# Moving an attention block from one chunk's down phase into the next chunk's up phase, with one cast on GpSimd

## Chip, cores and metric

One Trainium2 chip, one core. The metric is the device time of one execution in microseconds (us), the median of the runs. TensorE is called PE, VectorE DVE, ScalarE ACT, GpSimd POOL and SyncE SP, as in the profile.

## What is computed

```python
def _attn_ref(q, k, v):                       # (8, 8, 576, 64) each
    scores = scale * np.matmul(q, k.transpose(0, 1, 3, 2))
    gamma = 1.0 - 2.0 ** (-5.0 - np.arange(H))
    rel = pos[:, None] - pos[None, :]
    Dmat = np.where(rel >= 0, gamma[:, None, None] ** rel[None, :, :], 0.0)
    return np.matmul(scores * Dmat[None], v)

def _moe_ref(x, w_in, w_out):                 # x (4608, 512), w_in (512, 2048), w_out (2048, 512)
    h = x @ w_in
    g = h * (1.0 / (1.0 + np.exp(-1.702 * h)))
    return (g @ w_out)

x = attn_out.transpose(0, 2, 1, 3).reshape(B * S, H * D)
out = _moe_ref(x, w_in, w_out)
```

Attention has a decay per head in place of a softmax, so a sequence can be walked in pieces of 64 tokens with a running state (the sum of k times v). Its output, 4608 tokens of 512 features, goes through a two-layer network with a gate function between the layers.

## The kernel before

**Units, blocks, chunks.** A unit is 128 tokens with all 8 heads; there are 36. Every ninth unit (8, 17, ...) holds the last 64 tokens of two sequences and updates no state. Two units, 2j and 2j+1, make attention block j. Four units make a chunk, which the network takes at a time; there are 9 chunks. Chunk c needs x of blocks 2c and 2c+1.

**Attention of a block.** `scores` (L505) multiplies keys and queries into the PSUM banks C and D; `scores_out` (L514) masks them on DVE into `pm`. `state_both` (L434) forms the state updates of both halves of a unit in the banks K and E; `state_sum` (L447, L449) adds them up on DVE in `stm` (float32), and `state_cast` (L458) turns them into bf16 in `kv`. `block(j)` then runs `inter` (L489: queries times `kv`) and the first half of `values` (L527: `pm` times the scaled values `vp`), calls `ahead(j + 1)` (the scores and states of the next block), and runs the second half of `values`. It hands back a list of DVE steps to be issued later: `x_out_pair` (L552, which writes x in `xT`) for block j, and the masks and state sums for block j+1. `scale_v` (L353) makes `vp` on DVE.

**Network of a chunk.** The up phase has 16 steps f: `up` (L564) is 4 matmuls of 512 columns, then the gate function on ACT (L569) into `gT`; the banks A and B take turns. `up_group` does two f for half a chunk (units `lo` to `hi`): 8 matmuls of 256 columns (L578), one gate call (L583). `Pair.sums` (L653, L657) adds and subtracts parts of `gT` on DVE, 5 instructions for 8 f. The down phase is `Pair.run`: seven products of 16 matmuls (L675) on the banks A and B, with copies out on ACT (L691) and additions on DVE (L694), and seven places, `hook(0)` to `hook(6)`, where `steady` issues attention work.

**Order.** Each engine runs its instructions in the order of the program, and a small recorder puts semaphore waits between engines. So `steady` writes the order by hand: what is issued at which hook or step decides what waits behind what. In the up phase of chunk c it issues block 2c+2 and in the down phase block 2c+3. Chunk 1 is different: its up phase runs in half-chunk groups and holds block 3, and its down phase holds blocks 4 and 5, both of chunk 2:

```python
if i == 3:
    now(rest); rest.clear(); cast_now()
    rest.extend(block(4, cast=False))
if i == 5:
    now(rest); rest.clear(); state_cast(10, 12)
    rest.extend(block(5, cast=False))
n = len(rest) if i == 6 else 2
now(rest[:n])
```

**Loads.** GpSimd issues the loads of q, k (cast to bf16 on the way, `kqn`, L234) and v (`vn`, L247). SP issues the stores (L600) and the DMA transposes of `kqn` into `kqT` (L399). At the start of chunk c the transposes of units 4c+6 to 4c+9 are issued on SP, and the loads of units 4c+10 to 4c+13 on GpSimd, these after the transpose of unit 4c+9 has landed.

Of the kernel before, what the change touches and what calls it, by code (L numbers as in the profile page):

```python
# [29 lines left out]
class Program:  # L30
# [10 lines left out]
    def op(self, eng, fn, reads=(), writes=(), dma=None, ndma=1, after_ops=()):  # L41
        o = Op()
        o.eng, o.fn, o.dma, o.signal, o.count = eng, fn, dma, False, None
        o.idx = len(self.streams[eng]) + 1
        deps = {}
        for k in reads:
            for d in self.writers.get(k, ()):
                deps[id(d)] = (d, True)
        for k in writes:
            for d in self.writers.get(k, ()) + self.readers.get(k, ()):  # L50
                deps.setdefault(id(d), (d, False))
        known = self.known[eng]
        need = []
        for d, raw in deps.values():
            if d.dma is None:
                if d.eng == eng and dma is None and (eng == "pe" or not raw):
                    continue
                agent, val = d.eng, d.idx
            else:
                agent, val = d.dma, d.dval  # L60
            need.append((agent, val, d))
        for d in after_ops:
            need.append((d.eng, d.idx, d))
        need.sort(key=lambda x: -x[1])
        waits = {}
        for agent, val, d in need:
            if known.get(agent, 0) >= val:
                continue
            if agent in waits and waits[agent][0] >= val:
                continue  # L70
            waits[agent] = (val, d)
        pruned = []
        for agent, (val, d) in waits.items():
            if any(
                a2 != agent and d2.known.get(agent, 0) >= val
                for a2, (_, d2) in waits.items()
            ):
                continue
            pruned.append(d)
        for agent, (val, d) in waits.items():  # L80
            d.signal = True
            known[agent] = max(known.get(agent, 0), val)
            for a2, v2 in d.known.items():
                if v2 > known.get(a2, 0):
                    known[a2] = v2
        o.waits = pruned
        o.known = dict(known)
        if dma is None:
            o.known[eng] = max(o.known.get(eng, 0), o.idx)
        else:  # L90
            self.dma_count[dma] = self.dma_count.get(dma, 0) + 16 * ndma
            o.dval = self.dma_count[dma]
            o.known[dma] = o.dval
        self.streams[eng].append(o)
        for k in writes:
            self.writers[k] = (o,)
            self.readers[k] = ()
        for k in reads:
            self.readers[k] = self.readers.get(k, ()) + (o,)
        return o  # L100
# [60 lines left out]
def bass_retnet_parallel__then__act_gelu_quick_kernel(  # L161
# [10 lines left out]
    with es:  # L172
# [178 lines left out]
        def scale_v(u, eng="dve"):  # L351
            sl, ty = u % NLD, unit_info(u)[2]
            op(eng, lambda e: e.tensor_tensor(  # L353
                vp[u % NVP].ap(), vn[sl].ap(),
                vfac[:, ty, :, None].to_broadcast([P, H, DH]), ALU.mult),
               reads=[f"vn{sl}"] + VF, writes=[f"vp{u % NVP}"])
# [92 lines left out]
                op("dve", lambda e: e.tensor_tensor(dst, src, prev, ALU.add),  # L449
                   reads=[KB[a], f"stm{(i - 1) % 8}"], writes=[f"stm{i % 8}"])  # L450

        def state_cast(u0, u1):
            us = [u for u in range(u0, u1) if u < NU and unit_info(u)[1] < 2]
            if us:
                cast_range(2 * us[0], 2 * len(us))

        def cast_range(i0, n):
            op("act", lambda e: e.activation(  # L458
                kv[:, i0 % NKV : i0 % NKV + n, :, :], stm[:, i0 % 8 : i0 % 8 + n, :, :], AF.Copy),
               reads=[f"stm{(i0 + i) % 8}" for i in range(n)],  # L460
               writes=[f"kv{(i0 + i) % NKV}" for i in range(n)])

# [324 lines left out]
        def now(rest):  # L787
            for f in rest:
                f()
# [5 lines left out]
        def load(u, after=()):  # L795
            if u < NU:
                load_kq(u, 0, after=after)
                load_kq(u, 1, after=after)
                load_v(u, after=after)
# [139 lines left out]

        def steady():  # L940
            four = Pair(0, 2, 2)
            for c in range(1, NCH):
                if c == 1:
                    for u in (12, 13):
                        load(u)
                    for u in range(8, 14):
                        dma_transpose(u, ["vn1"])
                if c > 1:
                    for u in range(4 * c + 6, min(4 * c + 10, NU)):
                        dma_transpose(u)  # L950
                for u in range(4 * c + 10, 4 * c + 14):
                    load(u, after=[f"T{(4 * c + 9) % NQT}_0"])
                last = c == NCH - 1
                if c == 1:
                    for i in range(16):
                        f0, lo = 2 * (i % 8), 2 * (i // 8)
                        up_group(1, f0, 2, lo, lo + 2, turn())
                        if i == 0:
                            ahead(3)
                            now(ahead_out(3, False))  # L960
                        if i == 2:
                            state_cast(6, 7)
                        if i == 3:
                            state_cast(7, 8)
                        if i == 5:
                            now(block(3, lambda: None))
                            scale_v(8)
                            scale_v(9)
                        if i == 8:
                            scale_v(10)  # L970
                            scale_v(11)
                        if i in (11, 15):
                            four.sums(2 * (i - 11), 2 * (i - 11) + 8)
                else:
                    pair = Pair(3, 0, 1) if last else four
                    for f in range(NF):
                        up(c, f, b=turn())
                        if c == 2 and f in (3, 6):
                            state_cast(11 + f // 3, 12 + f // 3)
                        if f in (0, 2, 4, 6):  # L980
                            m = 4 * c + 6 + f // 2
                            if m < NU:
                                scale_v(m)
                        if f in (7, 15):
                            pair.sums(f - 7, f + 1)
                        if f == (10 if c == 2 else 9) and not last:
                            now(block(2 * c + 2))
                if last:
                    pair.run(c, lambda i: None)
                    for r, n0, n1, cp in ((1, 0, 512, "act"), (2, 0, 384, "act"), (2, 384, 512, "dve")):  # L990
                        b = turn()
                        for s in range(4):
                            down(c, r, s, b, n0, n1)
                        finish_unit(c, r, b, n0=n0, n1=n1, cp=cp, eng="sp" if n0 == 0 else "act")
                    break
                rest = []

                def hook(i):
                    if c == 1:
                        if i == 1:  # L1000
                            ahead(4)
                            rest.extend(ahead_out(4))
                            rest.extend([lambda: scale_v(12), lambda: scale_v(13)])
                        if i == 3:
                            now(rest)
                            rest.clear()
                            cast_now()
                            rest.extend(block(4, cast=False))
                        if i == 5:
                            now(rest)  # L1010
                            rest.clear()
                            state_cast(10, 12)
                            rest.extend(block(5, cast=False))
                    elif i == 0:
                        cast_now()
                    elif i == 2 and 2 * (2 * c + 3) < NU:
                        rest.extend(block(2 * c + 3))
                    n = len(rest) if i == 6 else 2
                    now(rest[:n])
                    del rest[:n]  # L1020
                    if i == 6:
                        cast_now()

                four.run(c, hook)
# [63 lines left out]
```

## Time and profile before

| | |
|---|---|
| median of 3 runs | 289.47 us (288.3 to 290.53) |
| profiled execution, its own time | 289.72 us |
| its span, first to last instruction | 287.9 us |
| mean granted clock of PE | 0.994 |
| PE busy | 279.0 us (97%) |
| DVE busy | 181.5 us (63%) |
| ACT busy | 130.1 us (45%) |
| GpSimd busy | 110.1 us (38%) |

Times inside the kernel are us from the start of the span. Busy time of PE counts matmuls from issue to modelled end, so it overlaps; a hole in it is certain, while a full row can still run at a lower clock. The granted clock is 1.00 when PE has its full clock. A row of the timeline shows start, duration, engine, line, operation and tiles, and in brackets the idle time of that engine before it with what ended it.

### The profile page before, as it was taken

What the parts mean: (1) busy time and instruction counts of PE and PEld (TensorE: products, weight loads), DVE (VectorE), ACT (ScalarE), POOL (GpSimd) and SP (SyncE); (2) the same over time, 40 slices, a digit from 0 to 9 for tenths busy, and PEclk for the clock granted to TensorE, in tenths of its full rate; (3) what the DMA queues carried; (4) which work ended last, traced back from release to release, by engine and by line L of the source; (5) the groups of instructions that cost most, each with busy time, mean ns of one, the idle gap of its engine ahead of it and who ended that gap; (6) DMA issues with size and microseconds to landing.
All of it is one profiled execution on the core that took longest, in us unless ns stands there. A gap on an engine that the chain in (4) does not pass through costs nothing.

```text
span 287.9 us, 8938 instructions
## 1 busy us (share of the span) xinstructions
PE 279.0 (97%) x4010; PEld 178.7 (62%) x4010; DVE 181.5 (63%) x350; ACT 130.1 (45%) x229; POOL 110.1 (38%) x141
## 2 busy tenths in 40 slices
PE   8999999999879999999999999999999999999996
PEld 6575455888653488348834883488348834883474
DVE  5953667568857967495949593859395928650240
ACT  7456334662117541654175417531754175306611
POOL 9999889000870860068006900670072000000000
PEclk9999999999979999999999999999999999999999
DMA  9999999999999990889398978892896070012012
GB/s 171 180 205 206 202 234 249 235 142 202 101 234 243 104 194 21 229 99 198 68 224 105 171 99 233 111 181 73 227 114 74 13 208 2 2 64 84 0 55 93
DMA packets 116790, 40.69 MB, mean 141 GB/s; under 512 B 104080, under 2 KB 109968, under 8 KB 116752
## 3 DMA queue, kind: packets, MB, share of 16 engines
q0 software_dynamic: 79712, 22.82, 68.7%
q1 hardware_dynamic: 36896, 17.24, 23.0%
q8 instruction: 31, 0.51, 0.7%
q10 hardware_dynamic: 144, 0.07, 0.1%
q14 instruction: 7, 0.06, 0.1%
HBM read 36.70 MB, written 9.44 MB: 160 GB/s over the span
## 4 chain that ended last, share of the span: by engine, by line
PE 82%; POOL 7%; DMA 6%; DVE 3%; ACT 1%; issue 0%; POOLq 0%
PE psA L564 17%; PE psB L564 17%; PE psA L675 16%; PE psB L675 15%; DMA vn<-in_v_dram 6%; POOL w_in_sb L269 3%; PE psB L578 3%; PE psA L578 2%; PE psA L590 2%; PE psB L590 2%; POOL kqn L234 2%; PE psX L489 2%; POOL vn L247 1%; POOL w_out_sb L276 1%; PE psC L505 1%; PE psK L434 1%
## 5 line engine op out<-in xcount | busy, mean ns | idle before, releaser
L234 POOL DMA_DIRECT2D kqn<-in_k_dram x39 | 35.0, 907 | 106.1 <-DMA kqT<-kqn 104.4
L564 PE MATMUL psA<-xT,w_in_sb 128*128 128x512 bf16 x240 | 61.7, 379 | 0.0
L564 PE MATMUL psB<-xT,w_in_sb 128*128 128x512 bf16 x240 | 61.7, 379 | 0.0
L653 DVE TENSOR_TENSOR gsum<-gT 128x1024 bf16<-128x1024 bf16 (+1 forms) x48 | 28.7, 654 | 48.3 <-ACT gT L569 45.6
L569 ACT ACTIVATE gT<-psB 128x512 bf16<-128x512 f32 x60 | 35.8, 597 | 28.6 <-PE psB L564 28.4
L569 ACT ACTIVATE gT<-psA 128x512 bf16<-128x512 f32 x60 | 35.8, 597 | 22.5 <-PE psA L564 22.3
L564 PEld LDWEIGHTS psB<-xT,w_in_sb 128*128 128x128 bf16 x240 | 19.7, 97 | 31.2 <-ACT gT L569 14.2
L564 PEld LDWEIGHTS psA<-xT,w_in_sb 128*128 128x128 bf16 x240 | 19.4, 97 | 30.9 <-ACT gT L569 14.3
L247 POOL DMA_DIRECT2D vn<-in_v_dram x40 | 37.0, 939 | 0.1
L234 POOL DMA_DIRECT2D kqn<-in_q_dram x37 | 33.4, 915 | 0.6 <-issue 0.6
L675 PE MATMUL psA<-wsum,gT 128*128 128x256 bf16 x240 | 29.8, 278 | 0.0
L458 ACT ACTIVATE kv<-stm 128x1024 bf16<-128x1024 f32 (+1 forms) x18 | 15.5, 863 | 29.9 <-DVE stm L449 29.9
L675 PE MATMUL psB<-wsum,gT 128*128 128x256 bf16 x240 | 28.9, 273 | 0.0
L675 PEld LDWEIGHTS psA<-wsum,gT 128*128 128x128 bf16 x240 | 23.6, 100 | 4.2 <-ACT gT L569 1.0
L675 PEld LDWEIGHTS psB<-wsum,gT 128*128 128x128 bf16 x240 | 23.1, 98 | 4.1 <-ACT gT L569 1.5
L353 DVE TENSOR_TENSOR vp<-vn,vfac 128x512 bf16<-128x512 f32 x36 | 23.0, 684 | 3.5 <-DMA vn<-in_v_dram 3.5
L552 DVE TENSOR_TENSOR xT<-psX,gq 128x512 bf16<-128x512 f32 x16 | 11.0, 689 | 18.3 <-PE psX L527 18.3
L657 DVE TENSOR_TENSOR gT<-gT 128x1024 bf16<-128x1024 bf16 (+1 forms) x32 | 19.5, 651 | 0.0
L691 ACT ACTIVATE osb<-psA 128x512 f32<-128x512 f32 (+1 forms) x12 | 7.0, 579 | 23.1 <-PE psA L675 23.1
L691 ACT ACTIVATE osb<-psB 128x512 f32<-128x512 f32 (+1 forms) x12 | 6.7, 562 | 19.1 <-PE psB L675 19.1
L675 PE MATMUL psA<-w_out_sb,gsum 128*128 128x256 bf16 x120 | 14.6, 273 | 0.4 <-issue 0.3
L675 PE MATMUL psB<-w_out_sb,gsum 128*128 128x256 bf16 x120 | 14.4, 273 | 0.0
(108 smaller groups left out, 433.9 us busy)
## 6 DMA issues: line engine op xcount, KB each, us to landing
vn<-in_v_dram POOLq DMA_DIRECT2D x32, 256.0 KB, 4.9
out_dram<-osb SPq DMA_DIRECT2D x31, 256.0 KB, 2.3
kqn<-in_k_dram POOLq DMA_DIRECT2D x31, 128.0 KB, 4.6
kqn<-in_q_dram POOLq DMA_DIRECT2D x31, 128.0 KB, 5.0
w_out_sb<-in_moe_w_out_dram POOLq DMA_DIRECT2D x4, 512.0 KB, 13.4
w_in_sb<-in_moe_w_in_dram POOLq DMA_DIRECT2D x8, 128.0 KB, 5.3
w_in_sb<-in_moe_w_in_dram POOLq DMA_DIRECT2D x4, 256.0 KB, 7.5
vn<-in_v_dram POOLq DMA_DIRECT2D x8, 128.0 KB, 4.2
```

Source lines behind the costliest of these rows:

```text
L234: e.dma_start(kqn[sl][p0 : p0 + n, which, :, :], src[b, :, s0 : s0 + n, :].rearrange("h p d -> p h d"),)
L247: e.dma_start(vn[sl][p0 : p0 + n, :, :], v[b, :, s0 : s0 + n, :].rearrange("h p d -> p h d"))
L353: op(eng, lambda e: e.tensor_tensor(vp[u % NVP].ap(), vn[sl].ap(), vfac[:, ty, :, None].to_broadcast([P, H, DH]), ALU.mult), reads=[f"vn{s ...
L458: op("act", lambda e: e.activation(kv[:, i0 % NKV : i0 % NKV + n, :, :], stm[:, i0 % 8 : i0 % 8 + n, :, :], AF.Copy), reads=[f"stm{(i0 + i ...
L564: op("pe", lambda e, a=a: e.matmul(bank[b][:, n0:n1], w_in_sb[:, a, P * f : P * f + P], xT[c % 2][:, a, n0:n1], start=(a == 0), stop=(a == ...
L569: op("act", lambda e: e.activation(gT[:, f, n0:n1], bank[b][:, n0:n1], AF.Gelu_apprx_sigmoid), reads=[b], writes=[f"g_{f}_{j}" for j in ra ...
L578: op("pe", lambda e, a=a, f=f, i=i: e.matmul(bank[b][:, n * i : n * i + n], w_in_sb[:, a, P * f : P * f + P], xT[c % 2][:, a, P * lo : P * ...
L590: op("pe", lambda e, f=f: e.matmul(bank[b][:, 0 : n1 - n0], gT[:, f, P * r : P * r + P], w_out_sb[:, f, n0:n1], start=(f == 0), stop=(f == ...
L653: op("dve", lambda e, n=n, x=x, y=y: e.tensor_tensor(gsum[:, n, f0 // 2 : f1 // 2, 0 : self.n], a(*x), a(*y), ALU.add), reads=g(*x) + g(*y ...
L657: op("dve", lambda e, x=x, y=y: e.tensor_tensor(a(*x), a(*x), a(*y), ALU.subtract), reads=g(*x) + g(*y), writes=g(*x))
L675: op("pe", lambda e, x=x, y=y, t=t, s=not more and t == 0 and k == 0, z=k == NF // 2 - 1: e.matmul(bank[b][:, 256 * t : 256 * t + 256], x, ...
L691: op("act", lambda e: e.activation(dst[0], src[0], AF.Copy), reads=src[1], writes=dst[1])
```

## The change

Block 5 leaves the down phase of chunk 1. Chunk 2's up phase now runs in 16 half-chunk groups as chunk 1's does, first for units 8 and 9, then for 10 and 11, and issues block 5 after three groups and block 6 after ten. The sums and the cast of block 4's state are issued at hook 1, ahead of its masks (which go out at hook 2). The cast of units 12 and 13 becomes one instruction on GpSimd, where two stood on ACT. The loads of units 18 to 21 are issued after it, and `scale_v` of units 12 and 13 is issued after the first group.

```diff
+        def cast_range(i0, n, eng="act"):
+            dst, src = kv[:, i0 % NKV : i0 % NKV + n, :, :], stm[:, i0 % 8 : i0 % 8 + n, :, :]
+            op(eng, lambda e: e.activation(dst, src, AF.Copy) if eng == "act" else e.tensor_copy(dst, src),
...
+            def loads_ahead(c):
+                for u in range(4 * c + 10, 4 * c + 14):
+                    load(u, after=[f"T{(4 * c + 9) % NQT}_0"])
...
-                for u in range(4 * c + 10, 4 * c + 14):
-                    load(u, after=[f"T{(4 * c + 9) % NQT}_0"])
+                if c != 2:
+                    loads_ahead(c)
...
+                elif c == 2:
+                    for i in range(16):
+                        f0, lo = 2 * (i % 8), 2 * (i // 8)
+                        up_group(2, f0, 2, lo, lo + 2, turn())
+                        if i == 0:
+                            scale_v(12)
+                            scale_v(13)
+                        if i == 2:
+                            now(block(5, cast=False))
+                            state_cast(12, 14, "pool")
+                            loads_ahead(2)
+                        if i in (4, 5, 6, 7):
+                            scale_v(10 + i)
+                        if i == 9:
+                            now(block(6))
+                        if i in (11, 15):
+                            four.sums(2 * (i - 11), 2 * (i - 11) + 8)
...
                     for f in range(NF):
                         up(c, f, b=turn())
-                        if c == 2 and f in (3, 6):
-                            state_cast(11 + f // 3, 12 + f // 3)
...
-                        if f == (10 if c == 2 else 9) and not last:
+                        if f == 9 and not last:
                             now(block(2 * c + 2))
...
                         if i == 1:
                             ahead(4)
-                            rest.extend(ahead_out(4))
-                            rest.extend([lambda: scale_v(12), lambda: scale_v(13)])
+                            out4 = ahead_out(4)
+                            now(out4[2:])
+                            cast_now()
+                            rest.extend(out4[:2])
                         if i == 3:
-                            now(rest)
-                            rest.clear()
-                            cast_now()
                             rest.extend(block(4, cast=False))
-                        if i == 5:
+                        if i == 6:
                             now(rest)
                             rest.clear()
                             state_cast(10, 12)
-                            rest.extend(block(5, cast=False))
...
-                    n = len(rest) if i == 6 else 2
+                    n = len(rest) if i == 6 else 0 if i == 1 else 2
```

More of the change, by code (lines that the diff above doesn't have):

```diff
@@ L450, in state_sum, with state_cast @@
                    reads=[KB[a], f"stm{(i - 1) % 8}"], writes=[f"stm{i % 8}"])
-        def state_cast(u0, u1):
+        def state_cast(u0, u1, eng="act"):
             us = [u for u in range(u0, u1) if u < NU and unit_info(u)[1] < 2]
             if us:
[L455 to L459, printed above, removed]
+                cast_range(2 * us[0], 2 * len(us), eng)
+        def cast_range(i0, n, eng="act"):
+            dst, src = kv[:, i0 % NKV : i0 % NKV + n, :, :], stm[:, i0 % 8 : i0 % 8 + n, :, :]
+            op(eng, lambda e: e.activation(dst, src, AF.Copy) if eng == "act" else e.tensor_copy(dst, src),
                reads=[f"stm{(i0 + i) % 8}" for i in range(n)],
```

## The prediction

> **What bounds the kernel now.** The first part of the page says how full TensorE (PE) is, and the table by stage says where it is not. The stages are chunk 1's down phase (three rows: 65.0 to 78.5, the hole, what follows it), chunk 2's up phase (85.7 to 101.1), and then, for comparison, the up and the down phase of chunk 3, which has no such edges.
>
> ```profile
> PE 279.0 (97%) x4010; PEld 178.7 (62%) x4010; DVE 181.5 (63%) x350; ACT 130.1 (45%) x229; POOL 110.1 (38%) x141
> ```
>
> ```profile
> core 0: us, PE busy (x) PEld busy (x) DVE busy (x) ACT busy (x) POOL busy (x), PEclk, DMA share, GB/s
> 65.00:78.50 13.50, 12.54 (x266) 10.77 (x264) 11.26 (x20) 2.91 (x5) 5.75 (x7) 1.00 0.97 155
> 78.50:81.30 2.80, 0.29 (x7) 0.12 (x6) 2.59 (x5) 1.06 (x1) 2.80 (x5) 1.00 1.69 198
> 81.30:85.70 4.40, 4.40 (x141) 3.69 (x142) 1.34 (x3) 0.00 (x0) 3.49 (x6) 0.61 1.68 248
> 85.70:101.10 15.40, 15.40 (x186) 6.34 (x184) 12.98 (x24) 9.78 (x17) 6.33 (x8) 1.00 1.12 174
> 114.95:130.16 15.21, 15.21 (x194) 6.28 (x192) 10.19 (x18) 8.96 (x15) 5.01 (x6) 1.00 0.86 172
> 130.16:143.63 13.47, 13.47 (x234) 11.97 (x233) 10.19 (x18) 3.37 (x6) 5.55 (x7) 1.00 1.08 121
> ```
>
> PE is the bound nearly everywhere: in chunk 3 it is busy for all 15.21 and all 13.47 us. Chunk 1's down phase takes 20.7 us (65.0 to 85.7), with 2.5 us empty in the hole, and behind the hole the granted clock is 0.61 where all other rows have 1.00. Next, the timeline: PE at its two waits, then ScalarE (ACT), then VectorE (DVE). A bracket holds the idle time before a row and what ended it.
>
> ```profile
> 73.97 0.21 PE L489 MATMUL psX<-kqT,kv 64*64 64x64 bf16 x1 [0.96 <-ACT kv L458]
> 81.30 0.21 PE L489 MATMUL psX<-kqT,kv 64*64 64x64 bf16 x1 [2.51 <-ACT kv L458]
> ```
>
> ```profile
> 72.80 0.60 ACT L691 ACTIVATE osb<-psB 128x512 f32<-128x512 f32 x1 [1.15 <-PE psB L675]
> 73.29 0.62 ACT L458 ACTIVATE kv<-stm 128x512 bf16<-128x512 f32 x1
> 80.19 1.06 ACT L458 ACTIVATE kv<-stm 128x1024 bf16<-128x1024 f32 x1 [6.27 <-DVE stm L449]
> ```
>
> ```profile
> 72.36 0.42 DVE L447 COPY stm<-psK 128x256 f32<-128x256 f32 x1
> ...
> 78.67 0.69 DVE L694 TENSOR_TENSOR osb<-psB,osb 128x512 f32<-128x512 f32 x1 [0.27 <-PE psB L675]
> 79.28 0.41 DVE L449 TENSOR_TENSOR stm<-psK,stm 128x256 f32<-128x256 f32 x1
> 79.73 0.42 DVE L449 TENSOR_TENSOR stm<-psE,stm 128x256 f32<-128x256 f32 x1
> ```
>
> Both PE waits are one chain: the state sums on DVE (`stm`), the cast on ACT (`kv`), then `inter` (L489), which opens an attention block. Block 4 lost 0.96 us because its cast stood behind the second output copy (72.80) and its sums behind two masks. Block 5 lost 2.51 us because its sums come after the output additions that wait for product 6 and its cast (1.06 us) follows them; no matmul lies between. ACT was idle for 6.27 us before that cast, so it is order and not load.
>
> **The clock behind the hole.** In the chain that ended last, the product after block 5 is "83.02 2.82 PE psA L675 x16" where its neighbours take 1.75: 1.07 us lost to the clock. Block 5 itself takes 1.65 us (81.30 to 82.95). So a hole of 2.5 us was enough here, and the 1.07 us is counted as gained when the hole goes. The Trainium skill (TensorE: Matmul & The Clock Gate, Part 1) puts the loss of the clock after at least one idle window of about 3.4 us; by that rule this hole would have cost no clock, and the gain below would be 1.1 us smaller.
>
> **The change, part by part.** (1) Block 4's sums and cast are issued at hook 1, ahead of the masks: sums after the `wtmp` addition (68.85 + 0.60), so 69.45 to 70.3, and the cast to about 71.0, just in time for the output copy at 71.05. The masks follow to 71.7, and block 4 needs them at about 72.9. The 0.96 us go. The `scale_v` of units 12 and 13 leave DVE here (2 x 0.6 us).
>
> (2) Block 5 leaves the down phase. What remains there is like chunk 3's down phase (13.47 us, one block of the same size) plus the scores and states of units 8 and 9 at hook 1 (0.50 us in the chain, 68.66 to 69.16) and one restart of 0.1. So 14.1 us instead of 20.7: -6.6. By pieces: 0.96, 2.73 (78.57 to 81.30), 1.65 for the block, 1.07 for the clock, 0.2 of small change. The up phase then starts at 79.1, and needs only units 8 and 9, whose x is ready at about 75.2.
>
> (3) Chunk 2's up phase gets block 5 and becomes 16 groups of 8 matmuls of 256 columns. Such groups in chunk 1 take 0.87 us each in the chain; the old ones take 0.86. Two blocks at 1.3 each (chunk 3's, 123.84 to 125.14, restart included): 16 x 0.87 + 2 x 1.3 + 0.1 = 16.6 to 16.7 us, against 15.4: +1.3. Two ACT casts that delayed geluing by about 0.3 us in all are gone in this.
>
> (4) Block 5 comes after three groups, at 81.8. Its cast now has cover: sums end at 78.9, the cast runs on ACT from 78.95 to 80.0, before the first gelu is due (80.1). That cover is the three groups (2.6 us); without it the 1.1 us of the cast would show again. Masks and `scale_v` 12 and 13 end at 82.2, and their first reader stands at about 82.5. The second half of x is written by 84.4; group 8 needs it at about 87.6.
>
> (5) The cast of units 12 and 13 goes to GpSimd. Its sums end at about 86.0 and GpSimd has issued its loads by 84.8 (last one below), so it starts at 86.0; block 6 asks for it at 89.3. It has 3.3 us. No row shows a GpSimd copy. Lower bound: its iotas take 134 ns for 5 and 237 ns for 128 columns, thus about 1.0 us for 1024. Upper bound: DVE's 0.68 us for 512 columns with two SBUF inputs, doubled, and held up for the four `scale_v` beside it (2.4 us): 3.8 us, 0.5 over its slack. I take 2 us, nearer the iota, the only GpSimd compute rows: no cost; 0 to 0.5 for the range. The Trainium skill (GPSIMD Engine Reference, Performance versus the Vector engine) speaks against the move: GpSimd takes about twice DVE's time in elementwise work and shares its SBUF interface with two-input DVE instructions. By its 2.6 cycles per element at 1.2 GHz the cast would be an estimated 2.2 us, which leaves the sum as it is.
>
> (6) Loads and queues. Behind the cast on GpSimd stand the 12 loads of units 18 to 21, but these wait for the transposes of unit 17 anyway, as now:
>
> ```profile
> 83.27 1.52 POOL L247 DMA_DIRECT2D vn<-in_v_dram x2
> 94.77 0.90 POOL L234 DMA_DIRECT2D kqn<-in_k_dram x1 [9.98 <-DMA kqT<-kqn]
> ```
>
> The loads of units 14 to 17 do not move, while their readers move 5 us ahead. The last `vn` lands at 88.7 (issued 83.9, 4.8 us), and `scale_v` of unit 17 now wants it at 89.2. On SP the four stores and the transposes of units 14 and 15 move from 86.6 and later into 78 to 83, beside these loads. Price: none at best; at worst all are served first, two more stores at about 0.7 and two transposes at 1.1 (they land 1.1 apart in a row), so 88.7 + 3.6 = 92.3. Behind that `scale_v`, DVE has 4 vector writes, 4 sums and two rounds of gate sums (10 x 0.6) before the `wtmp` addition, which the fourth product waits for: on time it ends at 101.5 and is asked for at 102.2. So a landing up to 90.5 is free, each later us costs one, at worst 1.8. I take 90 and cost 0.1.
>
> **Sum.** -6.6 + 1.3 + 0.1 = -5.2 us. From chunk 2's products on, each phase is full of PE work as before, so it only shifts. The profiled execution took 289.72 us (span 287.9 and 1.8 around it): 284.5. It lay 0.25 us above the median of 289.47, so for a median I say 284.3.
>
> **Rivals.** (A) The forecast: 284.3, own range 283.0 to 285.5.
> (B) DVE becomes the bound at chunk 2's end, since late loads push its queue: for it speaks that DVE is busy for 12.98 of 15.40 us there already and gets two masks, two x writes and two `scale_v` more (6 x 0.6 = 3.6 us), so some 16.6 us of work in a phase of 16.7; against it, that step 6 still leaves it 0.7 us to spare where PE first needs it. With the worst landing 1.8 us are lost: 286.2; with a product slowed as behind the hole, 1.1 more: 287.3.
> (C) The moved work is hidden anyway, because chunk 3 then waits for its loads: these start at 94 either way and landed by 109.3, while chunk 3's up phase moves from 115 to 109.7. Its transposes wait for stores until about 110, so about 0 to 2 us, 284.3 to 286.3. The time between speaks against it.
> (D) The other side: GpSimd's copy is far slower than any row suggests, so PE stands at block 6. Each us over 3.3 costs one, and a long hole costs the clock again (1.07). It decides from 3.3 + 5.2 - 1.1 = 7.4 us on; at 11 us the kernel would take 289.5 + 7.7 - 5.2 + 1.1 = 293.1. For it: no row has this operation. Against it: none of GpSimd's groups, issues included, has a mean over 0.94 us.
>
> **How the numbers follow.** A 0.70, B 0.15, C 0.09, D 0.06. The three runs spread by 0.4% to either side, so about 1% (2.9 us) is what can be told from no change: faster by more than that means below 286.6. All of A, two thirds of B and most of C lie there, 0.88; within 1% are the rest of these and a mild D, 0.08; slower 0.04. Range: from 282.8 (A less the 1.2 by which the lowest run lies under the median, and 0.3 for the readings) to 287.3 (B's end).
>
> **What would show it.** Right: no PE wait at L489 between 72 and 82, a granted clock of 1.00 there, chunk 1's down phase near 14.1 us and chunk 2's up phase near 16.7. Wrong: a PE wait on GpSimd at block 6 near 89 (step 5), `scale_v` waiting for `vn` beyond 90.5 with PE waiting for DVE near 102 (step 6), or an up phase over 17.2 without waits (step 3). A clock below 1.00 anywhere after 80 would mean that a hole has only moved.

## The result: slower, and the profile after

| | before | after |
|---|---|---|
| median | 289.77 us (288.3 to 290.53, 4 runs) | 298.15 us (296.3 to 299.76, 4 runs) |
| profiled execution, its own time | 289.72 us | 298.32 us |
| its span | 287.9 us | 296.4 us |
| mean granted clock of PE | 0.994 | 0.977 |

The ratio is 1.0273, with a 95% interval from 1.0224 to 1.0321: 2.7% slower, where 1.8% faster was forecast. The first part of the page does not show why. PE's busy time even rises by 2 us, in part because matmuls at half the clock count as busy for longer:

```profile
PE 281.1 (95%) x4074; PEld 186.5 (63%) x4074; DVE 181.5 (61%) x350; ACT 129.4 (44%) x227; POOL 111.2 (38%) x142
```

The table by stage does, with the columns as in the prediction. Its rows are chunk 1's down phase, chunk 2's up phase in three rows, and chunk 2's down phase:

```profile
65.40:79.51 14.11, 14.11 (x283) 12.39 (x282) 11.50 (x21) 3.05 (x6) 4.61 (x6) 1.00 0.80 133
79.51:92.20 12.69, 10.70 (x224) 8.74 (x221) 8.40 (x15) 6.99 (x11) 8.46 (x11) 1.00 1.71 199
92.20:105.85 13.65, 6.76 (x129) 5.08 (x130) 5.91 (x11) 1.19 (x2) 2.39 (x3) 0.50 1.22 102
105.85:108.65 2.80, 2.80 (x27) 2.29 (x26) 2.61 (x5) 1.79 (x3) 2.80 (x4) 1.00 1.47 164
108.65:122.60 13.95, 13.95 (x229) 12.18 (x228) 9.78 (x17) 3.97 (x6) 5.39 (x7) 1.00 1.08 131
```

The first row is the forecast to the tenth: chunk 1's down phase takes 14.1 us, with no hole and a full clock. Then chunk 2's up phase takes 29.1 us (79.51 to 108.65) where 16.7 were forecast, and for 13.65 us of it the clock is 0.50. Most of the loss is here: the two phases together take 43.25 us against 36.11 before, 7.1 more, of the 8.5 us by which the span grew. Another 0.9 us is a wait in chunk 4, at 173.72 (its kind is treated below).

PE's waits in that stretch, from its timeline:

```profile
92.49 0.26 PE L489 MATMUL psX<-kqT,kv 64*64 64x64 bf16 x1 [2.28 <-issue]
95.44 0.26 PE L505 MATMUL psC<-kqT 64*64 64x64 bf16 x1 [2.37 <-DMA kqT<-kqn]
100.10 0.26 PE L505 MATMUL psC<-kqT 64*64 64x64 bf16 x1 [4.23 <-DMA kqT<-kqn]
```

All three are in block 6: one in the middle of its `inter` (L489), for which the view names no cause ("issue"; more on it below), and two in its `ahead(7)`, whose scores (L505) read the transposed keys and queries of units 14 and 15. They add up to 8.9 us of the 12.4 us over the forecast. For the other 3.5 there is the half clock: PE was busy for 6.76 us at 0.50, an estimated 3.4 us more than at 1.00. The chain that ended last goes through the transposes instead of the state sums (start, duration, what). The landing times of the transposes issued between 78 and 108 us say the same; in the kernel before they were 2.7/2.8/3.8 (issued between 60 and 130 us):

```profile
82.18 2.67 SPq L399
84.84 0.05 issue
84.90 0.02 SPq L116
84.91 0.03 issue
84.94 15.11 DMA kqT<-kqn
100.05 0.04 issue
100.10 0.26 PE psC L505
```

```profile
DMA to landing us min/median/max: 4.0/13.2/15.1
```

Three of the four took 13.1 to 15.1 us; the fourth, issued at 99.08, when the loads had all but landed, took 4.0. The loads beside them are as late: the last `vn` (unit 17), issued at 86.10, lands at 99.86, and DVE stands twice for some 5 us before `scale_v`, in front of block 6's masks:

```profile
94.00 0.69 DVE L353 TENSOR_TENSOR vp<-vn,vfac 128x512 bf16<-128x512 f32 x1 [4.87 <-DMA vn<-in_v_dram]
99.88 0.69 DVE L353 TENSOR_TENSOR vp<-vn,vfac 128x512 bf16<-128x512 f32 x1 [5.19 <-DMA vn<-in_v_dram]
```

The view of the DMA queues from 78 to 105 us has, for each queue, its packets, MB and the time of its packets as a share of 16 engines. q0 carries GpSimd's loads, q1 SP's stores and transposes. First the kernel before, then the changed one:

```profile
q0 software_dynamic: 12724, 3.07, 106.2%
q1 hardware_dynamic: 4800, 2.10, 31.4%
```

```profile
GB/s 81 208 303 172 311 222 251 288 309 289 216 190 244 326 216 95 188 102 70 11 22 103 129 171 178 135 139 146 77 104 101 40 229 116 9 171 97 24 0 0
...
q0 software_dynamic: 7573, 1.96, 90.1%
q1 hardware_dynamic: 4800, 2.10, 56.0%
```

The same 4800 packets on q1 occupy 1.8 times as long, and one of q0 takes 1.4 times as long (90.1% / 7573 against 106.2% / 12724). In the row of GB/s a slice is 0.675 us: from 90.2 to 92.2 us the core moved 11 to 70 GB/s, while transposes and loads were both outstanding. In these 2 us the two do not just share one rate: 35 GB/s together, where the kernel before moves 201 with the transposes alone (90.1 to 94.4) and 152 with loads alone (95.0 to 109.0). Over the whole flight of the slowest transpose (84.94 to 100.05) it was 140.

GpSimd's cast, whose time the prediction could only bound (1.0 to 3.8 us), came out close to the lower bound:

```profile
86.78 1.19 POOL L459 CAST kv<-stm 128x1024 bf16<-128x1024 f32 x1
```

### The profile page after: what moved, and what is told of

Read it like the earlier page. It is cut to its first block, busy times and chain, and to the rows that moved or that the text cites. A ratio compares the mean times of both kernels' runs of the same rounds, so it can differ in the third digit from the quotient of the medians.

```text
span 296.4 us, 9067 instructions
## 1 busy us (share of the span) xinstructions
PE 281.1 (95%) x4074; PEld 186.5 (63%) x4074; DVE 181.5 (61%) x350; ACT 129.4 (44%) x227; POOL 111.2 (38%) x142
## 4 chain that ended last, share of the span: by engine, by line
PE 77%; DMA 11%; POOL 7%; DVE 2%; SPq 1%; issue 1%; ACT 0%; POOLq 0%
PE psA L675 16%; PE psB L675 15%; PE psA L564 14%; PE psB L564 14%; DMA vn<-in_v_dram 6%; DMA kqT<-kqn 5%; PE psB L578 4%; PE psA L578 4%; POOL w_in_sb L269 2%; PE psA L590 2%; PE psB L590 2%; POOL kqn L234 2%; PE psX L489 1%; POOL vn L247 1%; POOL w_out_sb L276 1%; PE psC L505 1%
## 5 line engine op out<-in xcount | busy, mean ns | idle before, releaser
L564 PE MATMUL psA<-xT,w_in_sb 128*128 128x512 bf16 x208 | 53.5, 379 | 0.0
L564 PE MATMUL psB<-xT,w_in_sb 128*128 128x512 bf16 x208 | 53.4, 379 | 0.0
L569 ACT ACTIVATE gT<-psB 128x512 bf16<-128x512 f32 x52 | 31.0, 597 | 21.5 <-PE psB L564 21.5
L569 ACT ACTIVATE gT<-psA 128x512 bf16<-128x512 f32 x52 | 31.0, 597 | 19.3 <-PE psA L564 19.2
L564 PEld LDWEIGHTS psB<-xT,w_in_sb 128*128 128x128 bf16 x208 | 16.9, 97 | 27.1 <-ACT gT L569 12.4
L564 PEld LDWEIGHTS psA<-xT,w_in_sb 128*128 128x128 bf16 x208 | 16.8, 97 | 26.7 <-ACT gT L569 12.4
L675 PE MATMUL psA<-wsum,gT 128*128 128x256 bf16 x240 | 28.8, 273 | 0.0
L459 ACT ACTIVATE kv<-stm 128x1024 bf16<-128x1024 f32 (+1 forms) x16 | 14.3, 894 | 32.5 <-DVE stm L449 32.5
L578 PE MATMUL psB<-xT,w_in_sb 128*128 128x256 bf16 x160 | 22.3, 286 | 0.0
L578 PE MATMUL psA<-xT,w_in_sb 128*128 128x256 bf16 (+1 forms) x168 | 20.8, 270 | 0.5 <-DVE xT L542 0.3
L583 ACT ACTIVATE gT<-psB 128x512 bf16<-128x512 f32 x20 | 11.9, 596 | 19.2 <-PE psB L578 19.1
L578 PEld LDWEIGHTS psB<-xT,w_in_sb 128*128 128x128 bf16 x160 | 15.4, 103 | 3.4 <-ACT gT L583 0.2
```

Source lines behind the costliest of these rows:

```text
L459: op(eng, lambda e: e.activation(dst, src, AF.Copy) if eng == "act" else e.tensor_copy(dst, src), reads=[f"stm{(i0 + i) % 8}" for i in ran ...
L564: op("pe", lambda e, a=a: e.matmul(bank[b][:, n0:n1], w_in_sb[:, a, P * f : P * f + P], xT[c % 2][:, a, n0:n1], start=(a == 0), stop=(a == ...
L569: op("act", lambda e: e.activation(gT[:, f, n0:n1], bank[b][:, n0:n1], AF.Gelu_apprx_sigmoid), reads=[b], writes=[f"g_{f}_{j}" for j in ra ...
L578: op("pe", lambda e, a=a, f=f, i=i: e.matmul(bank[b][:, n * i : n * i + n], w_in_sb[:, a, P * f : P * f + P], xT[c % 2][:, a, P * lo : P * ...
L583: op("act", lambda e: e.activation(gT[:, f0 : f0 + nf, P * lo : P * hi], bank[b][:, 0 : n * nf].rearrange("p (f t) -> p f t", f=nf), AF.Ge ...
L675: op("pe", lambda e, x=x, y=y, t=t, s=not more and t == 0 and k == 0, z=k == NF // 2 - 1: e.matmul(bank[b][:, 256 * t : 256 * t + 256], x, ...
```

## The experiments

**Theory 1**: the transposes of units 14 to 17 are now in flight beside the loads of 14 to 17 (and the stores are queued in front of both), and this overlap slows each of them several times over; PE stands at block 6 and loses its clock. **Theory 2**: the cast on GpSimd, or what it holds up, is at fault. **Theory 3**: the four stores that moved beside the loads fill the DMA engines by themselves. In the diffs "after" and "before" are the kernels of this case; e3 builds on e2, and e5, e6 and e9 on e3.

**e1, the cast back on ACT** (after):

```diff
-                            state_cast(12, 14, "pool")
+                            state_cast(12, 14)
```

> The changed kernel with the cast of units 12 and 13 back on ACT (one instruction, same place in the program); all else as changed. Theory 1 (the DMA transposes of units 14 to 17 run beside the loads of units 16 and 17, and both nearly stand still): no change, 296 to 300 us, transposes still landing over 10 us after issue, loads of unit 17 landing over 10 us after issue. Theory 2 (the GpSimd copy, in the middle of the loads, disturbs them or GpSimd's queue): the stretch is gone, about 284 to 286 us. Theory 3 (the four stores that moved beside the loads fill the DMA engines): no change.

Measured 298.49 us, ratio to before 1.0262 (1.0143 to 1.0381): as slow as after. The transposes still land up to 15.7 us after their issue and PE waits 2.08 and 6.96 us for them. So theory 2 falls as the cause of the late landing. That the time is the same is in part chance: PE also waits 2.72 us at 88.25 for a gate call that stands behind the cast on ACT, and not at all for instruction issue in block 6.

**e2, the transposes of chunk 2 wait for the last of the loads** (after):

```diff
                     for u in range(4 * c + 6, min(4 * c + 10, NU)):
-                        dma_transpose(u)
+                        dma_transpose(u, ["vn5"] if c == 2 else ())
```

> The changed kernel, with the transposes of units 14 to 17 made to wait until the last load (v of unit 17) has landed; stores and cast stay where they are. Theory 1: loads land 4 to 6 us after issue, the last near 90 to 91, transposes land 3 to 4 us after issue, those of units 14 and 15 near 94 to 95; block 6 asks for them at 90, so PE still waits 4 to 5 us there and loses 1 to 2 us to its clock: 288 to 291 us. Theories 2 and 3: the loads still land 10 us and more after issue, so everything comes later still: 298 us or more.

Measured 294.55 us, 1.0125 (1.0057 to 1.0193). Transposes take 2.8 us in the median again and the loads 3.6 to 7.9, although the four stores still lie beside these, so theory 3 falls. The time is a miss: the first transpose is issued only at 92.74, so block 6 waits 4.93 and 0.93 us for units 14 and 15, and the clock is at half from 95.2 to 102.0. The slow landing is cured by taking the overlap away; the place of the reader is then what costs.

**e3, the reader moved too** (e2): block 6 is issued without `ahead(7)`, which follows five groups later.

```diff
-                        if i in (4, 5, 6, 7):
+                        if i in (4, 5, 6):
                             scale_v(10 + i)
                         if i == 9:
-                            now(block(6))
+                            now(block(6, lambda: None))
+                            scale_v(17)
...
+                        if i == 14:
+                            ahead(7)
+                            now(ahead_out(7))
```

> As the run before it, but the scores and states of units 14 and 15 leave block 6 and are issued after group 14 (near 94), where the transposes have landed under theory 1; the vp of unit 17 is made after block 6's x. Theory 1: no hole longer than 1 us and a granted clock of 1.00, 284 to 287 us, which is the gain that the prediction named. Theories 2 and 3: 295 us or more.

Measured 288.76 us, 0.9935 (0.9897 to 0.9973): faster than before, but short of the forecast. The table by stage of chunk 1's down and chunk 2's up phase:

```profile
67.70:81.80 14.10, 14.10 (x282) 12.38 (x281) 11.50 (x21) 3.05 (x6) 7.07 (x9) 1.00 1.00 141
81.80:98.95 17.15, 17.06 (x378) 14.07 (x376) 14.21 (x25) 9.98 (x16) 6.02 (x8) 1.00 1.10 191
```

31.25 us for the two phases against 36.11 before: the 4.9 us are there. In this execution, 1.5 us above the median of the run, they are lost outside: chunk 1's down phase starts 2.7 us later than before, and 2.5 us are given back after the two phases, most of it in this one wait in chunk 4's down phase, where nothing was edited:

```profile
165.61 0.22 PE L527 MATMUL psY<-pm,vp 64*64 64x64 bf16 x2 [2.12 <-issue]
```

**e4, the overlap alone, in the kernel before**: units 14 to 17 are transposed at hooks 4 and 5 of chunk 1, ahead of the stores.

```diff
-                if c > 1:
+                if c > 2:
                     for u in range(4 * c + 6, min(4 * c + 10, NU)):
...
+                    if c == 1 and i in (4, 5):
+                        for u in ((14, 15), (16, 17))[i - 4]:
+                            dma_transpose(u)
```

> The kernel before, with nothing of the change except that the transposes of units 14 to 17 are issued at hooks 4 and 5 of chunk 1's down phase, ahead of the stores, so near 79 to 88 beside the loads of units 15 to 17. Theory 1: transposes land 8 us and more after issue, loads of units 16 and 17 too, DMA traffic falls below 60 GB/s for some us; block 6 (near 95) waits and the time is 290 to 297 us. Theories 2 and 3: there is no GpSimd copy and no store more beside the loads, so the transposes land in 3 to 5 us and the time is 288 to 290 us.

Measured 290.49 us, 0.9984 (0.9948 to 1.002). The landing times go as theory 1 says: transposes take 7.5 us in the median and up to 9.6, the loads up to 10. The time does not, since their readers in that order come late enough: a slow transfer costs only where its reader stands close behind.

**e8, the overlap alone, elsewhere** (before): chunk 5's loads no longer wait for the transposes of their chunk.

```diff
-                    load(u, after=[f"T{(4 * c + 9) % NQT}_0"])
+                    load(u, after=["osb2_256" if c == 5 else f"T{(4 * c + 9) % NQT}_0"])
```

> The kernel before, with one wait moved: the loads of units 30 to 33 start after an output addition of chunk 4 (near 171) and no longer after the transpose of unit 29 (near 182), so that they run beside the transposes of units 26 to 29. Theory 1: those transposes, 2.8 us each without loads beside them, land 6 to 15 us after issue, the loads 6 to 12 us instead of 4 to 5; block 12 (near 181) waits for them, 291 to 297 us. Rival (the trouble belongs to chunk 1 and 2, where the queue of loads is behind from the start): transposes stay under 5 us, 288.5 to 291 us.

Measured 297.26 us, 1.0247 (1.0184 to 1.031). Nothing else of the change is in this kernel, and it loses nearly what the change lost, in the same form, in block 12 of chunk 5, where the transposes land in 9.7 to 11.2 us:

```profile
186.12 0.26 PE L505 MATMUL psC<-kqT 64*64 64x64 bf16 x1 [2.84 <-DMA kqT<-kqn]
188.91 0.26 PE L505 MATMUL psC<-kqT 64*64 64x64 bf16 x1 [2.37 <-DMA kqT<-kqn]
```

That settles that the overlap is the cause. It does not say how it acts: while transposes were in flight here (176.4 to 196.0) the core moved 180 GB/s, no less than the kernel before moves for transposes alone (165, 177.0 to 181.8) and loads alone (140, 182.2 to 197.5). In e8 the two may simply share one rate, so that each transfer lands later. Stores stood in front of the transposes here too, so their share is the next question.

**e7, the transposes ahead of the stores** (after, with e4's edit; their overlap with the loads stays):

> The changed kernel with the transposes of units 14 to 17 issued at hooks 4 and 5 of chunk 1's down phase, ahead of the four stores on SP; the loads beside them are the same. Theory 1 (transposes beside loads, whatever the stores do): transposes and loads still land 8 to 15 us after issue, PE waits 3 us or more at block 6, 292 to 299 us. Rival (it takes the four stores in front as well): transposes land in 3 to 6 us, PE waits under 1.5 us, 285 to 289 us.

Measured 290.84 us, 1.003 (1.0004 to 1.0055), between the two expectations. The transposes now land in 3.8 to 8.4 us and PE waits for one of them only, 2.56 us. The late `vn` shows at the end of the phase as well, where PE waits 0.64 and 0.46 us for DVE in chunk 2's products. The first two transposes are issued at 81.07 and 85.00, close to the 82.18 and 84.94 of after, so it is the order: stores behind the transposes, two of them behind the loads as well (96.57 and later), are worth about 7 us of the loss. The rest of the overlap still eats the whole gain.

**The waits called issue.** In the trace a third queue (q8, "instruction") moves packets in step with PE's instructions, 16 KB for about every 256 of them. Count PE's records in pieces of 256: the waits called issue of 0.2 us and more after chunk 1, in all runs, stand at place 182 to 193 of a piece, 1.2 to 1.6 us after such a packet landed. So one edge of a piece lies there. The long waits stand where it falls in or behind an attention block, 256 instructions that PE issues in 1.1 us (before, 123.77 to 124.85). The Trainium skill (Runtime: NRT & Kernel Launch, Instruction fetch mechanics) states blocks of this size and calls the cost of crossing one "mostly hidden"; here up to 2.3 us were not. The longest one, in block 6 of after, is for the most part the overlap's work too: its packet took 1.89 us (the median of that run is 1.0) and lay in the 2 us of low traffic. In e2, e3 and e7, where PE's instructions up to there are the same, that packet took 0.9 to 1.0 us and there is no such wait; in e5 it is 0.35. The length also varies by execution: at one and the same instruction in chunk 4 it was 0.66 to 2.12 us (after, e1, e2, e3, e7). The theory for the next four runs (theory 4 in the expectations) is that the place of these ends decides where a wait appears.

**e6, the ends moved** (e3): 24 matmuls fewer, each with its weight load, in the start-up burst of PE, and nothing else.

```diff
-            warm_quads(NQUAD)
+            warm_quads(NQUAD - 24)
```

> The split version with 24 of the 57 small warming matmuls at the very start left out, so that all later PE instructions lie 48 places earlier in the stream; nothing else. Theory 4: the wait of about 2 us in chunk 4 is gone or under 0.3 us (other edges may get one), 286 to 288.5 us. Rival: the wait stays, 288 to 290 us. A later release of the clock at the start could cost up to 1 us in both.

Measured 288.19 us, 0.9935 (0.9902 to 0.9968). The wait of 2.12 us in chunk 4 is gone, as expected, and one of 1.57 us stands in chunk 5 at 191.81, before the same line L527. The two phases take 31.31 us.

**e10, the same edit in the kernel before**, with 23:

```diff
-            warm_quads(NQUAD)
+            warm_quads(NQUAD - 23)
```

> The kernel before with 23 fewer instructions in TensorE's start-up burst, and nothing else. Theory (edges of pieces of code): the edge of chunk 3's down-phase block comes to the end of an attention burst, and a wait called issue of 1 to 2 us appears there, near 136 us, while the 0.27 us wait at 108.6 us goes: 290.5 to 291.5 us. Rival (the place of the edges does not matter): no such wait, 289.5 to 290 us.

Measured 291.06 us, 1.0051 (1.0025 to 1.0077). The wait appears at the line that was named, smaller than expected, and the one of 0.27 us at 108.6 is gone:

```profile
137.98 0.22 PE L527 MATMUL psY<-pm,vp 64*64 64x64 bf16 x2 [0.65 <-issue]
```

The time rises by more than this wait; another of 0.44 us appears in chunk 1's up phase, at 56.6, and chunk 1's down phase starts 1.05 us later than before in all (66.05). Where the rest of that comes from is not shown.

**e5, fewer half-chunk groups** (e3): only steps 0 to 9 run in groups, and chunk 2's last six steps are whole again.

```diff
                     for i in range(16):
-                        f0, lo = 2 * (i % 8), 2 * (i // 8)
-                        up_group(2, f0, 2, lo, lo + 2, turn())
+                        if i < 10:
+                            up_group(2, 2 * (i % 5), 2, 2 * (i // 5), 2 * (i // 5) + 2, turn())
+                        else:
+                            up(2, i, b=turn())
...
```

The sums of `gT` move with them, to i == 8 and i == 15.

> The split version (transposes after the loads, scores and states of units 14 and 15 after group 14) with half-chunk groups only for f 0 to 9 of chunk 2 and whole-chunk steps for f 10 to 15: 24 matmuls and weight loads less. Theory 4 (PE waits 0.9 to 2.1 us for its own instructions in chunk 4's fourth attention burst, at the same instruction in all changed kernels, because 64 more matmuls put the edge of a 16 KB fetch at the end of a burst of 220 short instructions): the edge now comes 24 matmuls later, among the long products, the wait there is gone or under 0.3 us, and the time is 1 to 2 us under the split version: 286 to 288 us. Rival (the wait there has another cause, such as slow DMA traffic at that time): the wait stays, 288 to 290 us.

Measured 289.53 us, 0.9995 (0.9966 to 1.0023): a miss. The shorter program moves the ends again, and issue waits of 0.35, 0.65 and 1.54 us stand at 90.7, 164.6 and 193.3; two waits of 0.5 us on transposes come on top. Whether fewer groups are better by themselves is not told by this run.

**e9, the ends put where no block ends** (e3), and chunk 3's block one step later, since e3 waits there 0.57 us for a transpose:

```diff
-            warm_quads(NQUAD)
+            warm_quads(NQUAD + 11)
...
-                        if f == 9 and not last:
+                        if f == (10 if c == 3 else 9) and not last:
```

> The split version (block 6 without its successor at i == 9, the value scaling of unit 17 and the scores of block 7 later, transposes after the loads) with two more edits: 35 more instructions of TensorE's start-up burst than that version (NQUAD + 11 instead of NQUAD - 24 against the shifted one), which move the edges of the 256-instruction pieces of code away from the ends of the attention bursts in every down-phase block, and chunk 3's block 8 one group later (f == 10 instead of 9), after its transpose has landed. Theory (waits called issue are fetches of code at a piece's edge that falls at the end of an attention burst): no issue wait above 0.3 us anywhere after chunk 1, no wait on a transpose in chunk 3, and of the 4.8 us that the two phases gained all but about 1 us is kept: 284.5 to 286.5 us. Rival (the issue waits come from something else that the split version brings, such as the loads' order): one or two of 1 to 2 us remain, 288 us or more.

Measured 286.57 us, 0.9896 (0.9857 to 0.9934): the fastest of all, 1.0% under before, a little above the expected range. The issue waits after chunk 1 are 0.2 us at most; one of 0.44 us stands in chunk 1's up phase, at 55.70. Two rows of PE's waits (what waits, for what: us in all, times, longest):

```profile
PE psC L505 <- DMA kqT<-kqn: 0.8, 1, 0.8
...
PE psA L675 <- issue: 0.2, 1, 0.2
```

The 0.8 us are block 7's scores at 96.9, which still come just ahead of their late transposes; chunk 3 no longer waits for one. What the runs keep of the gain, from the starts of the phases:

| | before | after | e6 | e9 |
|---|---|---|---|---|
| start of chunk 1's down phase | 65.00 | 65.40 | 65.79 | 65.97 |
| from there to chunk 2's down phase | 36.11 | 43.25 | 31.31 | 32.33 |
| from there to the end of the span | 186.8 | 187.8 | 188.9 | 186.6 |

## Why the prediction was wrong

**Steps 1 and 2 held.** Both waits at L489 went, the clock stayed at 1.00, and the down phase took 14.1 us as summed. That a hole of 2.5 us can cost the clock held as well, against the rule of the Trainium skill that the prediction cites (TensorE: Matmul & The Clock Gate, Part 1): in e7 one of 2.56 us did. But length alone does not decide: in e1 the wait of 2.72 us up to 88.25 left the clock at 1.00. With block 6's three waits in after it was at half for 13.65 us.

**Step 3 was short by about 0.5 us.** Without waits for transfers, chunk 2's up phase took 17.15 us (e3) where 16.6 to 16.7 were summed; e3's block 6 is in two pieces there.

**Steps 4 and 5 held.** No PE wait for ACT or GpSimd shows at blocks 5 and 6. GpSimd's copy took 1.19 us, next to the bound from the iota (1.0), and the one from DVE was far off. It is also about half of the 2.2 us estimated from the Trainium skill (GPSIMD Engine Reference, Performance versus the Vector engine), whose 2.6 cycles per element are for two inputs where this copy has one. Only the last 0.24 us of it ran beside a `scale_v`, so what such work costs it is not shown. Rival D falls.

**Step 6 failed**, and with it the sign. The step saw that the transposes and stores move beside the loads, and bounded the price by serving them one after another: a landing of `vn` at 92.3 at worst, 1.8 us on PE, with 0.1 taken. Two things are wrong in that. First, the worst case took the times from rows where transposes and loads run apart. Measured beside each other, the `vn` landed at 99.86, and three of the four transposes needed 13 to 15 us instead of 2.8. Without the transposes the loads kept near the step's times: in e2, with the four stores beside them, that `vn` landed 5.7 us after its issue, against 4.8 before. (It was issued at 87.02 there and at 86.10 in after, where the step had 83.9: the loads came 2 to 3 us later too.) Second, the step named one reader, `scale_v` of unit 17. The transposes have one as well, the scores of units 14 and 15 in block 6, and it was moved too; it was never priced, and it is where PE stood for 6.6 us. The 2.28 us ahead of them, for instructions, and the half clock follow from the same crowd.

The trace of before had a hint against the bound that was not read so: from 65 us on it hardly has transposes and loads in flight together, since the loads of a chunk wait for its last transpose. Only around 88 us they touch: the transpose issued at 87.51, beside the last loads and two stores, took 3.60 us. The prediction took that wait as mere order. The Trainium skill (DMA: Bandwidth & Descriptors, Rules for kernel authors) says "A transpose next to ordinary DMAs needs nothing"; its row is about right results, and on time e8 says otherwise (9.7 to 11.2 us where 2.8 were usual).

**The rivals.** B's mechanism (late loads push DVE into chunk 2's products) is in e7, with 1.1 us. C's kind of wait is in e3 and e6, 0.5 to 0.6 us in chunk 3, for transposes. None of them held the one that decided.

**The sum itself** was nearly right once the overlap is gone: -4.8 and -4.9 us over the two phases (e6, e3) against -5.2. What the best version keeps of it at the end is about 3 us (e9): its two phases are 3.8 us shorter, with 0.8 us of waiting for a transpose in them, and chunk 1's down phase starts 1.0 us later, 0.44 of it the issue wait at 55.70. In e3 and e6 the long issue waits take 2.12 and 1.57 us.

**What stays open:** why the two kinds of transfer slow each other. The runs show that they do, at which traffic, and that stores in front make it worse. A shared rate may be enough in e8 (180 GB/s); it is not for the 2 us at 35 GB/s in after. No run takes the loads' cast or the size of their packets apart.

## What to carry to other kernels

A transfer that is moved beside others is not priced by its time alone: look for the place in the trace where the two kinds already run together, and if there is none, take that for a warning and ask what keeps them apart. For each transfer that moves, name its own first reader and the slack in front of it, not only the readers of its neighbours. And when a long kernel gets a wait in a stage that nobody edited, look whether pieces of its program now end at a burst of short instructions before blaming the stage.

## What the hardware showed unexpectedly

- DMA transposes beside GpSimd's casting loads: landing after 9.7 to 11.2 us (e8), up to 15.1 in after, both with stores in front; 3.8 to 8.4 ahead of the stores (e7); 2.8 apart. For 2 us of it the core of after moved 11 to 70 GB/s.
- A wait that goes with the fetch of PE's program costs 0.2 to 2.3 us where an edge of its pieces of 256 instructions falls in or behind an attention block, and removing or adding 11 to 24 start-up matmuls moves that cost through the kernel. A crowded DMA lengthens it: in block 6, 2.28 us in after, none in e2, e3 and e7.
- PE's clock was cut by holes of 2.3 to 2.6 us, but not by one of 2.72 us in e1. The single hole of e7 (2.56 us) cost half the clock from 94.3 to 97.7 us; the stretches at half clock behind holes lasted 3.4 us (before, e7), 6.8 (e2, e8), 10.2 (e1) and 13.65 (after), so 3.4 us or a multiple.
